# Attention into a token-mixing MLP on one Trainium2 core: one hand-written order of steps exchanged for another

## The chip, the core and the metric

The kernel runs on one NeuronCore of a Trainium2 chip. The core has five engines that run side by side, each with its own queue of instructions in program order: TensorE (PE in the profile, with its weight loads as PEld) multiplies matrices into PSUM; VectorE (DVE), ScalarE (ACT) and GpSimd (POOL) work elementwise; SyncE (SP) issues transfers. GpSimd, SyncE and ScalarE can all issue DMAs. An engine waits for another through semaphores.

The metric is the device time of one execution in microseconds. Before the change it is 104.38 us, the median of three runs (104.2, 104.38 and 105.15). One more execution was taken with the profiler: 104.42 us.

## What is computed

Eight batches, eight heads, 576 rows and head size 64. Thirty-two learned queries `p` pack the keys and values of each head (first softmax), the real queries attend to the packed result (second softmax), and the output, put back to 576 rows of 512, goes through a token-mixing MLP.

```python
def sm_attn(qq, kk, vv):
    s = scale * np.matmul(qq, kk.transpose(0, 1, 3, 2))
    s = s - np.max(s, axis=-1, keepdims=True)
    a = np.exp(s)
    a = a / (np.sum(a, axis=-1, keepdims=True) + 1e-09)
    return np.matmul(a, vv)
p_packed = sm_attn(p, k, v)
out = sm_attn(q, p_packed, p_packed)
# x: (batch, 576, 8 * 64)
wq = x @ w_q
wk = x @ w_k
W_tok = (1 / sqrt(64)) * np.einsum('bsd,btd->bst', wq, wk)
mixed = np.einsum('bst,btd->bsd', W_tok, x)
return np.maximum(mixed, 0.0) @ w_out
```

Inputs and output are fp32; the kernel multiplies in bf16. It never forms `x` or the 576 x 576 matrix `W_tok`: it works with the packed products.

## The kernel before

The kernel has no loops over data in its body. It is a list of small steps, and a string `ORDER` (lines 13 to 57) names every step of all eight batches in the order in which the program issues them. The loop at lines 601 to 622 reads the string and calls one function for each name. An engine therefore does its own steps in the order of the string, and what one step needs from another engine makes it wait. Nothing reorders them.

A name reads `STEP.batch.part@engine=banks`: `RL.5.0@V` is step RL of batch 5, part 0, on VectorE (`V`; `A` is ScalarE, `P` GpSimd, `S` SyncE), and `=6,7` are the PSUM banks that a product goes to. There are eight banks; a product must wait until the step that reads the bank's earlier content is done. Steps without a letter have a fixed engine: products run on TensorE, `LD` on GpSimd's DMA queue, `ST`, `STF`, `STH` on SyncE's unless marked `@P` or `@A`.

What a batch goes through, in order of data:

- `LD.k`, `LD.v`, `LD.q`: loads through GpSimd's queue, cast from fp32 to bf16 on the way (lines 154 to 182). `k0` comes as `h0` and `g0`, `q0` and `q7` as two halves (`r`, `q`). Four buffers each (`NL`). `LD.O` loads `w_out`. Each load waits, on GpSimd, for the transfer that was issued eight before it.
- `KT` (VectorE): the keys transposed in blocks; `S1` (32 matmuls): scores of the packed queries; `X1` (ScalarE): their exponentials, in one buffer; `TE` (VectorE): these transposed.
- `PV` (36 matmuls): the weighted values and, through the ones that `SET.v0` to `SET.v3` write, the sums; `RC`, `PP`, `PT` (VectorE): reciprocal, normalized packed result, its transpose.
- `QK`, `QKE`, `QD`: the packed result times `w_q` and `w_k`, its eviction, and a copy on GpSimd.
- `QV` (VectorE): the queries transposed; `S2` (matmuls), `X2` (ScalarE): scores and exponentials of the second softmax, in parts `.0` to `.3`; `RS`, `RR` (VectorE): row sums and reciprocals, with `HA` on GpSimd for a first addition in batch 5; `AM` (mostly GpSimd): the normalization.
- `AT`, `AE`: the probabilities transposed on TensorE, and evicted.
- `WKQ`, `WE`, `GM`, `GE`, `Y`, `YE`, `MX` and `MR`, `RL` (or `RLF` by halves) and `RLR`: the mixing, each product with its eviction, ending with the ReLU.
- `OT`: four accumulating matmuls of 512 columns against `w_out` for 128 rows (`.0` to `.3`), and `.4` for the 64th rows of two batches together; `OE`, `OEF`: eviction to the output tile; `ST`, `STF`: its store, 512 KB or 256 KB. The last 128 rows of batch 7 are cut in two column parts (`OH`, `OEH`, `STH`), with the bounds in `OHC` (line 11).

`WARM.n=b` puts n times 128 columns of fp32 matmuls without use into bank b, as a filler while TensorE has nothing to do. `HOLD.v7` is a tiny transfer on SyncE's queue that waits for v7's landing, so that the stores behind it on that queue start after the loads.

The steps around the change: at the start, batch 0 runs alone with fillers, and batch 1's first scores begin. In the middle, `OT` of earlier batches is put between the steps of later ones. At the end, stores wait in SyncE's and GpSimd's queues.

Of the kernel before, what the change touches and what calls it, by code (L numbers as in the profile page):

```python
# [23 lines left out]
RS.1.2@V RR.1.2@V S2.1.1=2,3 X2.1.0@A RS.1.0@V RR.1.0@V WARM.1=6 PV.2.0=6,7 PV.2.1 X2.1.1@A RS.1.1@V RC.2@V  # L24
LD.v3 QD.1@P AM.1.2@P AT.1.2=4 RR.1.1@V AM.1.0@P WARM.5=5 AT.1.0=5 AM.1.1@P LD.k4 PP.2.0@V AE.1.2@A PP.2.1@V
PT.2@V QK.2=4 AE.1.0@A QKE.2@A QD.2@P QV.2.2@V LD.q3 LD.v4 AT.1.1=0 AE.1.1@A WKQ.1.0=2,3 WKQ.1.2 WKQ.1.1
WE.1.0@V S2.2.2=6,7 WE.1.1@A X2.2.2@A S2.2.3=4,5 X2.2.3@A GM.1=1 OT.0.0=2,3 GE.1@V Y.1=6,7 OT.0.1 YE.1@A
# [10 lines left out]
HOLD.v7 MR.3=0,1 RC.5@V PP.5.1@V OE.2.1@A MX.3.0=2,3 PP.5.0@V PT.5@V MX.3.1=6,7 RLR.3@A RL.3.0@A OT.3.4=0
RL.3.1@A AT.4.2=1 AE.4.2@A OEF.3.4@A QV.5.2@V AT.4.3=5 AE.4.3@V ST.1.4@P QK.5=4 QKE.5@V QD.5@P S2.5.2=2,3
X2.5.2@A KT.6.2@V S2.5.3=6,7 X2.5.3@A HA.5@P WKQ.4.0=0,1 WKQ.4.2 LD.q7 WKQ.4.1 WE.4.2@A OT.3.0=2,3  # L40
S1.6=4,5,6,7 X1.6.0@A GM.4=0 GE.4@V TE.6.0@V LD.r7 OT.3.1 X1.6.1@A TE.6.1@V Y.4=0,1 OE.3.0@A RS.5.4@V RR.5.4@V
PV.6.0=4,5 YE.4@A PV.6.1 MX.4.0=6,7 RC.6@V RL.4.0@A PP.6.0@V AM.5.3@P PP.6.1@V PT.6@V MX.4.1=2,3 AM.5.2@P
# [10 lines left out]
WE.7.1@A STF.6.2 OT.6.0=6,7 OT.6.1 GM.7=0 OE.6.0@V OT.5.1 OE.5.0@V ST.5.1@P GE.7@A Y.7=4,5 OT.6.3 OEF.6.3@V
ST.6.0 STF.6.3 YE.7@A ST.5.0 MR.7=6,7 RLR.7@A MX.7.0=4,5 RLF.7.0.1@A RLF.7.0.0@V MX.7.1=2,3 RLF.7.1.0@A
OT.7.4=0 OEF.7.4@A ST.7.4 RLF.7.1.1@V OT.7.1=6 OEF.7.1@V OT.7.0=7 STF.7.1 OT.7.2=1 OEF.7.0@A OH.7.0=0 STF.7.0
OEF.7.2@A STF.7.2 OEH.7.0@V STH.7.0 OH.7.1=5 OEH.7.1@A STH.7.1@A
"""


# [1 line left out]
def kernel(  # L61
# [46 lines left out]
    def bank(n, shape, dt=fp32):  # L108
        if isinstance(n, list):
            assert n[1] == n[0] + 1  # L110
            ap = ps_all[:, n[0]:n[1] + 1].rearrange("a k n -> a (k n)")
# [12 lines left out]
        return ap.rearrange(f"a ({' '.join(names)}) -> a {' '.join(names)}", **dims)

    def copy(eng, o, i):
        if eng == "A":
            nc.scalar.activation(o, i, COPY)  # L128
        elif eng == "P":
            nc.gpsimd.tensor_copy(o, i)  # L130
        else:
            nc.vector.tensor_copy(o, i)  # L132
# [441 lines left out]
    def OH(b, h, eng, bk):  # L574
        n0, n1 = OHC[h]
        ps = T["oh", h] = bank(bk, [n1 - n0])
        for j in range(NJ):
            nc.tensor.matmul(ps, T["relu", b][:, j // 2, j % 2, 3 * P:4 * P], wout[:, j, n0:n1],
                             start=j == 0, stop=j == NJ - 1)
# [71 lines left out]
```

## Time and profile before

| | |
|---|---|
| runs, us | 104.2, 104.38, 105.15 |
| profiled execution, us | 104.42 |
| its span, us | 102.6 |
| granted TensorE clock, mean | 0.993 |
| instructions | 3594 |
| moved by DMA | 25.13 MB, 245 GB/s on average |
| share of 16 DMA engines, GpSimd's queue | 84.3% |
| share of 16 DMA engines, SyncE's and ScalarE's queues | 18.9% and 1.9% |

The span runs from the first to the last instruction of the profiled execution; the profiled time holds 1.8 us more that lie around it. Times in the views are counted from the span's start. A transfer's queue time isn't an engine's busy time: an engine is not counted as busy while it issues or waits. Matmul ends are modelled, and matmuls overlap, so the steps of the chain of waits tell better what a product costs than the length of its row.

### The profile page before, as it was taken

How to read it: one execution, taken by the hardware profiler on the slowest of the kernel's cores; microseconds unless marked ns; L12 is line 12 of the kernel's file. 1: busy time of each engine (PE TensorE's matmuls, PEld its weight loads, DVE VectorE, ACT ScalarE, POOL GpSimd, SP SyncE). 2: the span in 40 equal slices, each digit the busy share in tenths (PEclk: the TensorE clock that was granted, in tenths of full speed). 3: DMA queues.
4: the chain of work that ended last, by engine and by line, in shares of the span. 5: the costliest groups of instructions: out<-in, count | busy, mean ns of one | idle time of the engine just before them, and what ended most of it. 6: DMA issues, size and time to landing. Idle time of an engine off the chain costs nothing.

```text
span 102.6 us, 3594 instructions
## 1 busy us (share of the span) xinstructions
PE 93.2 (91%) x1536; PEld 55.1 (54%) x1536; DVE 73.5 (72%) x140; ACT 65.0 (63%) x111; POOL 53.1 (52%) x83
## 2 busy tenths in 40 slices
PE   5998999998699999999998899989999999999930
PEld 3896555465265633755636557544757565643420
DVE  4164376957979479888697979499999979249420
ACT  1320415178754767849977979887989897726430
POOL 5971877993039929724459493649724009300000
PEclk9999999999999999999999999999999999999997
DMA  1999999999999999999999999999999999997893
GB/s 18 234 230 207 211 215 209 207 210 213 203 212 207 214 209 209 213 210 207 212 210 208 211 212 204 216 211 205 250 250 387 412 413 409 417 388 294 346 370 127
DMA packets 13567, 25.13 MB, mean 245 GB/s; under 512 B 1072, under 2 KB 6448, under 8 KB 13552
## 3 DMA queue, kind: packets, MB, share of 16 engines
q0 software_dynamic: 9936, 17.04, 84.3%
q1 hardware_dynamic: 3056, 7.41, 18.9%
q10 hardware_dynamic: 560, 0.46, 1.9%
q8 instruction: 12, 0.20, 0.7%
q14 instruction: 3, 0.02, 0.1%
HBM read 30.15 MB, written 9.44 MB: 386 GB/s over the span
## 4 chain that ended last, share of the span: by engine, by line
PE 64%; DVE 9%; ACT 8%; DMA 7%; POOL 4%; issue 3%; DVEq 0%; POOLq 0%; ACTq 0%
PE ps L540 26%; PE ps L617 9%; DMA k_sb<-in_k_dram 7%; PE ps L373 5%; PE ps L315 4%; ACT e1T L293 4%; POOL a L405 4%; PE ps L282 3%; PE ps L419 3%; PE ps L446 3%; PE ps L467 3%; DVE rs L394 2%; PE ps L441 2%; PE ps L336 2%; DVE kT L237 2%
## 5 line engine op out<-in xcount | busy, mean ns | idle before, releaser
L540 PE MATMUL ps<-wout,relu 128*128 128x512 bf16 x124 | 30.6, 380 | 0.0
L405 POOL TENSOR_TENSOR a<-e,rr 128x256 bf16<-128x256 f32 (+2 forms) x18 | 19.5, 1099 | 16.4 <-DVE rr L399 6.4
L617 PE MATMUL ps<-o 128*128 128x128 f32 (+3 forms) x76 | 20.0, 410 | 1.2 <-DVE o L135 1.2
L540 PEld LDWEIGHTS <-relu 128*128 128x128 bf16 x124 | 10.7, 98 | 11.7 <-issue 1.1
L128 ACT ACTIVATE o<-ps 128x1024 f32<-128x1024 f32 (+2 forms) x13 | 11.3, 870 | 5.4 <-PE ps L540 5.2
L617 PEld LDWEIGHTS ps<-o 128*128 128x128 f32 x76 | 11.8, 217 | 5.2 <-issue 3.6
L503 ACT ACTIVATE relu<-ps 128x1024 bf16<-128x1024 f32 (+1 forms) x14 | 12.9, 966 | 1.1 <-PE ps L492 1.1
L293 ACT ACTIVATE e1T<-ps 128x576 bf16<-128x576 f32 x16 | 9.8, 655 | 5.2 <-PE ps L282 4.6
L378 ACT ACTIVATE e<-ps 128x256 f32<-128x256 f32 (+2 forms) x19 | 11.2, 622 | 2.5 <-PE ps L373 2.4
L394 DVE TENSOR_REDUCE rs<-e 128x16 f32<-128x512 f32 (+2 forms) x13 | 10.9, 841 | 2.3 <-ACT e L378 2.2
L173 POOL DMA_DIRECT2D v_sb<-in_v_dram x16 | 10.0, 629 | 4.2 <-DMA v_sb<-in_v_dram 1.6
L237 DVE STREAM_TRANSPOSE kT<-k_sb 128x1152 uint32<-128x1152 uint32 (+1 forms) x9 | 11.0, 1226 | 1.4 <-DMA k_sb<-in_k_dram 1.3
L237 DVE STREAM_TRANSPOSE qT<-q_sb 128x1152 uint32<-128x1152 uint32 (+1 forms) x10 | 11.0, 1104 | 0.0
L132 DVE COPY o<-ps 128x1024 f32<-128x1024 f32 (+2 forms) x7 | 6.7, 977 | 5.2 <-PE ps L540 2.7
L237 DVE STREAM_TRANSPOSE e<-e1T 128x288 uint32<-128x288 uint32 x16 | 7.4, 468 | 3.1 <-ACT e1T L293 2.6
L128 ACT ACTIVATE aT<-ps 128x128 bf16<-128x128 f32 (+2 forms) x11 | 5.0, 464 | 5.7 <-PE ps L419 3.3
L128 ACT ACTIVATE wkq<-ps 128x448 bf16<-128x448 f32 (+1 forms) x10 | 7.2, 729 | 1.8 <-PE ps L446 1.7
L315 PE MATMUL ps<-v_sb,e 64*64 64x192 bf16 x288 | 7.5, 245 | 0.8 <-DVE e L237 0.5
L315 PEld LDWEIGHTS <-e 64*64 64x64 bf16 x288 | 5.9, 107 | 2.6 <-DVE e L237 2.0
L373 PEld LDWEIGHTS <-qT 64*128 64x128 bf16 x320 | 5.4, 94 | 2.6 <-DVE qT L237 1.5
L446 PE MATMUL ps<-aT,pqk 128*128 128x256 bf16 (+1 forms) x48 | 6.8, 246 | 0.0
L373 PE MATMUL ps<-ppT,qT 64*128 64x64 bf16 x320 | 6.6, 190 | 0.1
(70 smaller groups left out, 131.5 us busy)
## 6 DMA issues: line engine op xcount, KB each, us to landing
v_sb<-in_v_dram POOLq DMA_DIRECT2D x16, 288.0 KB, 14.5
out_dram<-o SPq DMA_DIRECT2D x9, 512.0 KB, 8.9
k_sb<-in_k_dram POOLq DMA_DIRECT2D x7, 576.0 KB, 14.0
q_sb<-in_q_dram POOLq DMA_DIRECT2D x6, 576.0 KB, 13.5
out_dram<-o POOLq DMA_DIRECT2D x4, 512.0 KB, 9.0
out_dram<-o SPq DMA_DIRECT2D x5, 256.0 KB, 3.0
...
```

Of the source, the lines that this page charges most:

```text
L128: nc.scalar.activation(o, i, COPY)
L173: nc.gpsimd.dma_start(v_bufs[b % NL][halves(i), 0:7:2], src)
L237: nc.vector.transpose(o, i)
L293: nc.scalar.activation(e1T[:, x], T["s1", b][x].rearrange("a c m -> a m c"), EXP, scale=scale)
L315: nc.tensor.matmul(T["pv", b][halves(cc), i], lhsT, rhs, start=n == 0, stop=n == R - 1, skip_group_check=True)
L373: nc.tensor.matmul(ps[:, y, t - t0, i], lhsT, rhs, start=e == 0, stop=e == 1)
L378: nc.scalar.activation(e2[:, t0:t1].rearrange("a t (i y n) -> a y (t i) n", i=2, y=2), T["s2", b, c].rearrange("a y t i n -> a y (t i) n") ...
L394: nc.vector.tensor_reduce(rs[:, t0 * H:t1 * H], src, axis=AX, op=ADD)
L405: e.tensor_tensor(a2[:, t0:t1].rearrange("a t i (u l) -> a (t i u) l", l=L), e2v(b, c), T["rr", b][:, t0 * H:t1 * H].to_broadcast((P, (t1 ...
L503: nc.scalar.activation(o, i, RELU)
L540: nc.tensor.matmul(ps, lhsT, wout[:, j, :], start=j == 0, stop=j == NJ - 1)
L617: nc.tensor.matmul(bank(int(bk), [w]), warm[:, 0:P], rhs, start=True, stop=True)
```

## The change

Only `ORDER` and `OHC` differ. Every step of the computation is still there, with the same shapes; the order in the string, the engine of some evictions, and many banks are different. What changes, by stage:

- Start: the mask, the memsets of ones and the loads of k2, v1, q1, v2 stand differently among each other on GpSimd. Batch 0's parts 0 and 1 exchange places in `S2` to `AT`. `S1.1` comes before `WKQ.0`, `X1.1` before `WE.0`; `S1.2` before `GM.0`. `GE.0` goes to VectorE, `YE.0` to ScalarE, `RLR.0` to VectorE, `QKE.1` to ScalarE, `AE.1.0` to VectorE, `WE.1.0` to ScalarE. `TE.2.1` moves behind `PP.1.1`. The fillers add up to 77 units of 128 columns instead of 69; behind `QK.1` it is `WARM.6` instead of `WARM.3`.
- Loads: the order of the transfers on GpSimd's queue stays, but for the two halves of q7 (`r7` first) and the steps between them: `AM.2` before `LD.q4`, `AM.3` before `LD.v6`, `AM.4` and `QD.4` before `LD.v7`, `HA.5` and the loads of q7 before `QD.5`.
- Middle: `GM.2`, `Y.2` and `MX.2.1` come before the rest of batch 1's `OT`; `YE.2` and `RL.2.1` go to VectorE, `RLR.2` and `QKE.3` to ScalarE. `QK.5` moves behind `Y.4`; `AT.4` before `OT.3.4`; `GE.5` and `AE.6.2` go from ScalarE to VectorE.
- Stores: `ST.2.1` and, late, `ST.3.0`, `ST.5.1` and `ST.5.4` are on GpSimd's queue; before, `ST.1.1`, `ST.0.1`, `ST.3.0` early and `ST.5.1` late. SyncE's queue has the others in another order.
- End: batch 7's `AT`, `WKQ`, the last `OT` of batches 5 and 6 and their evictions change places and engines; the two column parts of the last rows exchange names.

The core of the diff (the start, the middle, and the end of the string):

```diff
-OHC = (0, 384), (384, 512)
+OHC = (384, 512), (0, 384)
...
-KT.1.2@V AM.0.1@P WARM.3=2 AT.0.1=7 AE.0.1@A AE.0.0@V WKQ.0.0=2,3 WKQ.0.2 WE.0.0@A LD.q2 WKQ.0.1 KT.2.2@V
-S1.1=0,1,4,5 WE.0.1@A GM.0=6 X1.1.0@A TE.1.0@V GE.0@A WARM.2=7 Y.0=2,3 YE.0@V S1.2=0,1,6,7 MR.0=2,3 X1.1.1@A
-TE.1.1@V MX.0.0=4,5 X1.2.0@A LD.O PV.1.0=0,1 TE.2.0@V PV.1.1 X1.2.1@A TE.2.1@V RC.1@V LD.k3 PP.1.0@V PP.1.1@V
-PT.1@V MX.0.1=6,7 QV.1.2@V RLR.0@A QK.1=2 QKE.1@V RL.0.0@A WARM.3=3 S2.1.2=4,5 S2.1.0=0,1 RL.0.1@A X2.1.2@A
+RR.0.0@V AM.0.0@P WARM.3=2 AT.0.0=2 KT.1.2@V S1.1=0,1,4,5 X1.1.1@A X1.1.0@A AE.0.0@V WKQ.0.0=6,7 WKQ.0.2
+WE.0.0@A KT.2.2@V WKQ.0.1 WARM.2=3 S1.2=2,3,4,5 WE.0.1@A GM.0=0 LD.q2 LD.O TE.1.0@V TE.1.1@V GE.0@V SET.v3@P
+LD.k3 X1.2.0@A TE.2.0@V LD.v3 WARM.2=1 Y.0=6,7 PV.1.0=2,3 PV.1.1 RC.1@V PP.1.0@V PP.1.1@V X1.2.1@A TE.2.1@V
+YE.0@A PT.1@V MR.0=0,1 RLR.0@V MX.0.0=4,5 RL.0.0@A MX.0.1=6,7 RL.0.1@A QK.1=2 QKE.1@A QD.1@P QV.1.2@V WARM.6=3
...
-WE.2.2@A OT.1.2=4,5 OT.1.3 PP.3.0@V PT.3@V QK.3=6 OE.1.1@A LD.q5 KT.4.2@V S1.4=0,1,2,3 GM.2=7 OT.1.0=4,5
-X1.4.1@A LD.k6 GE.2@A QKE.3@V X1.4.0@A QV.3.2@V TE.4.1@V Y.2=2,3 YE.2@A S2.3.2=6,7 X2.3.2@A S2.3.3=0,1
-X2.3.3@A MX.2.0=2,3 TE.4.0@V RL.2.0@A MR.2=6,7 RLR.2@V OT.1.1 MX.2.1=6,7 RL.2.1@A OE.1.0@A PV.4.0=0,1 QD.3@P
+RC.3@V PP.3.0@V OT.1.2=6,7 WE.2.2@A GM.2=0 GE.2@A KT.4.2@V S1.4=2,3,4,5 X1.4.1@A PP.3.1@V PT.3@V X1.4.0@A
+Y.2=0,1 YE.2@V OT.1.3 OE.1.1@A MX.2.1=0,1 QV.3.2@V RL.2.1@V LD.q5 TE.4.1@V QK.3=4 LD.k6 TE.4.0@V S2.3.2=2,3
+QKE.3@A X2.3.2@A S2.3.3=6,7 X2.3.3@A MX.2.0=4,5 OT.1.0=2,3 RS.3.4@V RR.3.4@V MR.2=0,1 PV.4.0=6,7 PV.4.1 RC.4@V
...
-OT.4.2=0,1 GM.5=4 TE.7.1@V OT.4.3 AT.6.3=5 X1.7.0@A TE.7.0@V GE.5@A OE.4.1@A AM.6.2@P AT.6.2=4 ST.2.0 Y.5=6,7
-YE.5@A ST.0.0 ST.3.1 PV.7.0=2,3 QV.7.1@V AE.6.3@V QV.7.0@V AE.6.2@A QD.6@P PV.7.1 RC.7@V PP.7.0@V PP.7.1@V
+TE.7.1@V X1.7.0@A OT.4.2=2,3 GM.5=4 GE.5@V TE.7.0@V QV.7.0@V OT.4.3 ST.1.1 OE.4.1@A AT.6.3=5 AM.6.2@P AT.6.2=4
+AE.6.2@V ST.0.0 Y.5=6,7 AE.6.3@V ST.4.0 PV.7.0=0,1 PV.7.1 RC.7@V PP.7.0@V QV.7.1@V YE.5@A MR.5=2,3 RLR.5@A
...
-RR.7.2@V MR.6=2,3 OT.5.3 RLR.6@V RL.6.0@V RL.6.1@A OE.5.1@A ST.4.1 AM.7.0@P OT.5.0=2,3 AM.7.2@P AT.7.0=4
-AE.7.0@A AT.7.1=5 AE.7.1@V AT.7.2=6 AE.7.2@V OT.6.2=0,1 OEF.6.2@A QD.7@P WKQ.7.0=4,5 WKQ.7.2 WKQ.7.1 WE.7.0@A
+AM.7.1@P RLR.6@V AM.7.0@P OT.5.3 OE.5.1@A RR.7.2@V OT.5.0=6,7 AT.7.1=4 RL.6.0@V AE.7.1@V AT.7.0=5 AE.7.0@V
+OT.6.2=0,1 OEF.6.2@V ST.3.0@P QD.7@P AM.7.2@P AT.7.2=2 WKQ.7.0=4,5 WKQ.7.1 AE.7.2@A STF.6.2 WKQ.7.2 WE.7.1@V
+WE.7.0@A OT.5.1 OE.5.0@A ST.5.1@P ST.5.4@P GM.7=0 OT.6.0=2,3 OT.6.1 OE.6.0@A ST.5.0 GE.7@V Y.7=4,5 OT.6.3
```

More of the change, by code (lines that the diff above doesn't have):

```diff
@@ L23 @@
-PT.1@V MX.0.1=6,7 QV.1.2@V RLR.0@A QK.1=2 QKE.1@V RL.0.0@A WARM.3=3 S2.1.2=4,5 S2.1.0=0,1 RL.0.1@A X2.1.2@A
[L24 to L27, printed above, removed]
@@ L38 @@
[L38 to L42, printed above, removed]
@@ L53 @@
[L53 to L56, printed above, removed]
+LD.g0 LD.v0 LD.r0 LD.q0 LD.k1 NC.0@V PX.0@V NC.1@A PX.1@V SET.aff@P SET.idb@V KT.0.0@V KT.0.1@V WC.1@P WC.0@P
@@ new lines @@
+PP.2.0@V PP.2.1@V PT.2@V QK.2=4 QKE.2@A AT.1.1=0 AE.1.1@A AE.1.0@V WKQ.1.0=6,7 WKQ.1.2 LD.k4 WE.1.0@A WKQ.1.1
+WE.1.1@A QV.2.2@V S2.2.2=2,3 X2.2.2@A S2.2.3=4,5 X2.2.3@A GM.1=1 GE.1@V OT.0.0=6,7 Y.1=2,3 YE.1@A OT.0.1
+OE.0.0@A MX.1.1=0,1 RS.2.4@V RL.1.1@A MR.1=4,5 RR.2.4@V QD.2@P KT.3.2@V OT.0.2=2,3 RLR.1@A OT.0.3 S1.3=6,7,0,1
+X1.3.0@A LD.q3 OE.0.1@V LD.v4 AM.2.2@P TE.3.0@V X1.3.1@A AM.2.3@P AT.2.2=4 LD.q4 LD.k5 OT.1.4=5 AT.2.3=6
+OEF.1.4@A MX.1.0=2,3 TE.3.1@V LD.v5 AE.2.3@V PV.3.0=0,1 AE.2.2@A RL.1.0@A PV.3.1 WKQ.2.0=4,5 WKQ.2.1 WKQ.2.2
@@ new lines @@
+LD.r7 X1.6.0@A OT.3.1 OE.3.0@A LD.q7 Y.4=0,1 ST.2.1@P TE.6.1@V TE.6.0@V YE.4@A ST.0.1 QK.5=2 QKE.5@A QD.5@P
+PV.6.0=4,5 PV.6.1 RS.5.4@V RR.5.4@V MX.4.0=6,7 RL.4.0@A RC.6@V PP.6.1@V MX.4.1=0,1 RL.4.1@A PP.6.0@V PT.6@V
+AM.5.3@P QV.6.2@V OT.3.2=2,3 OT.3.3 OE.3.1@V QK.6=5 QKE.6@A ST.3.1 S2.6.2=6,7 S2.6.3=0,1 X2.6.2@A X2.6.3@A
+MR.4=4,5 RLR.4@V AM.5.2@P AT.5.2=6 AE.5.2@A AT.5.3=7 AE.5.3@A OT.4.0=2,3 OT.4.1 OE.4.0@A WKQ.5.0=4,5 WKQ.5.2
+KT.7.2@V ST.1.0 RS.6.4@V WKQ.5.1 WE.5.2@A S1.7=0,1,6,7 ST.3.4 QD.6@P ST.2.0 RR.6.4@V AM.6.3@V X1.7.1@A
@@ L57 @@
+STF.7.2 STF.7.0 OH.7.0=5 OEH.7.0@A OEH.7.1@V STH.7.1@A STH.7.0
 """
```

36 lines of the change are left out of this document (18 added, 18 removed).

## The prediction

> **What bounds the kernel now.** I read the page's engine and DMA rows first, then the windows, then the end of the chain of waits. From the page, its busy times, its GB/s slices (2.56 us each) and its chain by engine:
>
> ```profile
> PE 93.2 (91%) x1536; PEld 55.1 (54%) x1536; DVE 73.5 (72%) x140; ACT 65.0 (63%) x111; POOL 53.1 (52%) x83
> ...
> GB/s 18 234 230 207 211 215 209 207 210 213 203 212 207 214 209 209 213 210 207 212 210 208 211 212 204 216 211 205 250 250 387 412 413 409 417 388 294 346 370 127
> ...
> PE 64%; DVE 9%; ACT 8%; DMA 7%; POOL 4%; issue 3%; DVEq 0%; POOLq 0%; ACTq 0%
> ```
>
> TensorE (PE) holds 64% of the chain. The GB/s row has two plateaus: about 210 while the loads arrive, and about 410 from slice 30 (77 us) on, when only stores flow. Up to about 77 us the arrival of the loads times each batch, and TensorE fills the rest with products of earlier batches. The windows (stretch, its length, busy time of PE, PEld, DVE, ACT and POOL, the clock, DMA share, GB/s) tell what binds afterwards:
>
> ```profile
> 70.00:80.00 10.00, 10.00 (x201) 6.30 (x199) 9.86 (x13) 8.78 (x16) 5.55 (x7) 1.00 1.11 283
> ...
> 78.70:84.30 5.60, 5.55 (x136) 3.84 (x134) 4.87 (x12) 5.32 (x12) 0.00 (x0) 1.00 1.03 410
> 84.30:88.00 3.70, 3.70 (x32) 1.83 (x30) 3.06 (x8) 2.97 (x5) 3.18 (x5) 1.00 1.02 409
> 88.00:91.00 3.00, 3.00 (x30) 1.77 (x29) 0.38 (x2) 1.52 (x4) 0.35 (x1) 1.00 1.04 420
> 91.00:94.00 3.00, 2.98 (x31) 1.19 (x29) 2.88 (x3) 1.07 (x4) 0.00 (x0) 1.00 0.76 303
> ```
>
> From 70 us on TensorE is never free for long, and VectorE (DVE) is busy 9.86 of 10 us in 70 to 80. The DMA share falls to 0.76 in 91 to 94 us, so the stores don't bind the last ten microseconds. The end of the chain of waits (start, length, what):
>
> ```profile
> 94.03 3.63 PE ps L540 x16
> 97.66 0.67 PE ps L578 x4
> ...
> 98.40 0.56 DVE o L132
> ```
>
> The last products run without a break to 98.3 us. An eviction, the last store and its landing make the rest of the 102.6 us span. So the end is TensorE's backlog plus some 4 us. Time is won only where TensorE idles less between 40 and 82 us, and lost wherever a feeder falls behind it there.
>
> **The start: batch 1's queries come later.** S1.1 and its exponentials move ahead of WKQ.0 and WE.0. TE.2.1 moves from before RC.1 to behind PP.1, and RLR.0 goes from ScalarE to VectorE, ahead of QV.1. The filler behind QK.1 grows from WARM.3 to WARM.6. Timeline (start, length, engine, line, what; in brackets the idle time before and its releaser), and two rows of the chain of waits:
>
> ```profile
> 24.98 0.94 PE L315 MATMUL ps<-v_sb,e 64*64 64x192 bf16 x36 [0.24 <-ACT e1T L293]
> 28.47 0.78 PE L373 MATMUL ps<-ppT,qT 64*128 64x64 bf16 x40
> ...
> 24.96 1.02 DVE L237 STREAM_TRANSPOSE e<-e1T 128x288 uint32<-128x288 uint32 x2 [0.34 <-ACT e1T L293]
> ...
> 27.08 1.34 DVE L237 STREAM_TRANSPOSE qT<-q_sb 128x1152 uint32<-128x1152 uint32 x1
> ...
> 49.58 0.42 DVE L505 TENSOR_SCALAR rem<-ps 128x256 bf16<-128x256 f32 x1 [0.58 <-PE ps L498]
> ...
> 13.15 1.49 PE ps L617 x4
> ...
> 27.21 0.41 PE ps L336 x8
> ```
>
> PV.1 waited 0.24 us for batch 1's and 2's exponentials; I credit all of it. Behind PV.1 on VectorE, QV.1 (27.08) now has half of the 1.02 (0.51, TE.2.1) and a 0.42 (RLR.0) ahead of it: 0.93 - 0.24 - 0.1 for overlapping starts = 0.6 us later, so it ends near 29.0. PT.1 has only TE.2.1 in front, 0.51 - 0.24 = 0.27, so QK.1 starts at 27.21 + 0.27 = 27.48; with its 0.41 and 1.49 of filler (the 13.15 row is a WARM.6) TensorE is free only near 29.3. Starts overlap a little, so S2.1 moves from 28.47 to about 29.2: **+0.75**. Bounds: +0.3 if PV.1 comes 0.5 earlier still, +1.0 if the credit fails.
>
> On GpSimd the memset of v2's ones now stands between QD.0 and the loads of v2, ahead of AM.0.2:
>
> ```profile
> 13.53 0.60 POOL L206 MEMSET v_sb<- 128x576 uint32 x1
> 17.53 0.62 POOL L405 TENSOR_TENSOR a<-e,rr 128x256 bf16<-128x256 f32 x1 [0.34 <-DVE rr L399]
> ...
> 39.92 0.48 PE L282 MATMUL ps<-kT,pT 32*32 32x288 bf16 x32
> ```
>
> 0.60 less the 0.34 of idle time is 0.26, and the longer filler WARM.8 (two units more, at 1.49/6 each = 0.5) lies over it: free; without that cover it is 0.26. The loads of k2, v1, q1 are issued a little later but keep their order, and the load queue has work without a pause (GB/s row), so they land as before. The mask and the ones of v1 and v3 are memsets that only change places: free. From S2.1 to S1.3 each step waits for the one ahead: S1.3, at 39.92 now, inherits +0.75.
>
> **Batch 2's products ahead of batch 1's.** Before S2.3 TensorE did OT.1.2, OT.1.3, QK.3, S1.4, GM.2, OT.1.0, Y.2; now OT.1.2, GM.2, S1.4, Y.2, OT.1.3, MX.2.1, QK.3. OT.1.0 leaves the path, MX.2.1 enters. YE.2 goes to VectorE, ahead of QV.3.
>
> ```profile
> 37.86 0.22 PE ps L492 x2
> ...
> 44.19 0.92 ACT L128 ACTIVATE wkq<-ps 128x896 bf16<-128x896 f32 x1 [0.93 <-PE ps L446]
> ...
> 23.81 0.42 DVE L486 TENSOR_SCALAR y<-ps 128x256 bf16<-128x256 f32 x1
> ...
> 46.67 1.37 DVE L237 STREAM_TRANSPOSE qT<-q_sb 128x1152 uint32<-128x1152 uint32 x1
> ...
> 48.54 0.67 PE ps L373 x32
> ```
>
> One OT is 3.63/4 = 0.91. The path loses 0.91 and gains 0.22: -0.69. GM.2 now follows WE.2.2 (0.92) with one OT (0.91) as its only cover: +0.1. TensorE would thus reach S2.3 at +0.75 - 0.69 + 0.1 = +0.16. But Y.2 and YE.2 (0.42) come before QV.3, and QV.3 starts at about 47.25, not 46.67; S2.3.3 also needs the bank that OE.1.1 empties. I take **+0.4** at S2.3.3 (48.54 now), between +0.16 and +0.75. The 0.69 is owed again behind it (OT.1.0 before PV.4), which the next stall must cover.
>
> ```profile
> 54.46 0.62 PE L419 MATMUL ps<-idb,a 128*128 128x128 bf16 x8 [0.45 <-POOL a L405]
> 57.22 0.49 PE L282 MATMUL ps<-kT,pT 32*32 32x288 bf16 x32 [0.32 <-DVE kT L237]
> 68.14 0.94 PE L315 MATMUL ps<-v_sb,e 64*64 64x192 bf16 x36 [0.47 <-DVE e L237]
> ...
> 62.94 0.34 PE ps L336 x8
> ```
>
> AT.3.3 idled 0.45 for AM.3.3; the owed work fills this, and AT.3.3 keeps about +0.45 as its VectorE chain does. The 0.32 before S1.5 remains, for KT.5 is as late as TensorE. In batch 4 AT.4 moves ahead of OT.3.4 and waits for AM.4.2, but S2.5 waits for QV.5 anyway: free while QV.5 is late. QK.5 (0.34) moves from before S2.5 into the 0.47 idle before PV.6: -0.1 after what the later TE.6 takes. PV.6 stands at **+0.35**.
>
> **VectorE's full stage.** GE.5 and AE.6.2 go from ScalarE to VectorE, which has no idle time there; QV.7.1 moves between PP.7.0 and PP.7.1.
>
> ```profile
> 77.77 0.31 ACT L128 ACTIVATE g<-ps 128x128 bf16<-128x128 f32 x1
> ...
> 66.73 0.29 DVE L132 CAST g<-ps 128x128 bf16<-128x128 f32 x1 [1.31 <-PE ps L467]
> 42.76 0.27 DVE L132 CAST aT<-ps 128x128 bf16<-128x128 f32 x1
> 81.07 0.31 DVE L237 STREAM_TRANSPOSE ppT<-pp 128x128 uint32<-128x128 uint32 x1
> 81.30 1.19 DVE L505 TENSOR_SCALAR relu<-ps 128x1024 bf16<-128x1024 f32 x1
> ...
> 82.11 0.41 PE L373 MATMUL ps<-ppT,qT 64*128 64x64 bf16 x16
> 82.86 0.53 PE L373 MATMUL ps<-ppT,qT 64*128 64x64 bf16 x24
> ```
>
> 0.29 + 0.27 = 0.56 more on VectorE; what leaves ScalarE (0.31 for GE.5) helps no one, since the waits there end with VectorE. RL.5.0 (81.30 + 1.19 = 82.49) empties the banks of S2.7.0, which starts near 83.0 (behind the first 8 of the 24 matmuls of the 82.86 row): cover 0.50. So 0.56 - 0.50 = 0.06 if TensorE is on time, and the whole 0.56 on top of VectorE's lag if TensorE isn't. With both 0.35 late: 0.4. I take +0.2 for the stage, a sum of **+0.55**. [...]
>
> **Stores and tail.** ST.3.0, ST.5.1 and ST.5.4 are issued late by GpSimd, ST.3.0 and QD.7 ahead of AM.7.2.
>
> ```profile
> 84.53 2.63 POOL L405 TENSOR_TENSOR a<-e,rr 128x512 bf16<-128x512 f32 x3 [6.35 <-ACT y L484]
> 87.10 0.29 POOL L130 COPY pqk<-pqk 128x128 bf16<-128x128 bf16 x1
> 87.68 0.66 POOL L561 DMA_DIRECT2D out_dram<-o  x1 [0.29 <-ACT o L128]
> ```
>
> AM.7 ran to 87.16; one issue (0.66) and QD.7 (0.29) ahead of AM.7.2 make it 0.95 later. AT.7.2 now stands behind OT.6.2, 0.91 of cover: hidden, and up to 0.95 late if the cover is gone. WKQ.7, GM.7, Y.7 and MX.7 keep the same products around them in another order, WE.7.1, GE.7 and YE.7 go to VectorE, which is nearly idle there (0.38 of 3 us in 88 to 91): 0. The last product is cut as before, 384 columns and then 128, with the two stores' queues exchanged: 0. Moving 0.75 MB of stores (ST.3.0, ST.5.4) to later and ST.5.0 ahead of ST.6.0 fills room that the DMA has at 91 us: 0. The two queues together moved 410 GB/s (78.7 to 84.3), SP's alone 409 (84.3 to 88): a second queue adds no rate. [...]
>
> **Sum.** The profiled execution took 104.42 us (span 102.6 and 1.8 around it; the median of the runs is 104.38). 104.42 + 0.75 - 0.40 + 0.20 = 104.97, so **105.0**. The runs spread from 104.2 to 105.15, so 1% (below 103.3, above 105.4) is about what a measurement can tell from no change.
>
> **Rivals.**
> Slower: the lag is not absorbed. Mechanism: QV.3 is held by YE.2 while VectorE is itself 0.75 late, so S2.3 gets 0.75 + 0.42 = +1.17 and every later query step queues behind it; the full stage adds 0.06 to 0.56. 104.42 + 1.17 + 0.2 = 105.8. It decides once QV.3 starts later than about 47.7. For it: VectorE's 9.86 of 10. Against: the 0.69 that leaves the path. With AM.7.2's cover gone too, up to 106.7.
> Faster: TensorE makes up the start, and the three stalls quoted (0.45 + 0.32 + 0.47 = 1.24) are all filled by moved products: 103.2. For it: QK.5 does fit the 0.47. Against: two of the three stalls are waits on chains through VectorE, which gets more work.
> No effect: S1.3 waits for k3's landing and the backlog hides the rest, and the stores' new queues do nothing: 104.4. For it: the 0.76 DMA share. Against: S1.3 had no idle time before it that could hide a lag.
>
> **Chances.** Forecast case 0.42, its own range 104.3 to 105.6, of which about a sixth (0.07) lies above 105.4; slower rival 0.35; faster 0.13; no effect 0.10. Faster by over 1%: 0.13. Within 1%: 0.35 + 0.10 = 0.45. Slower by over 1%: 0.35 + 0.07 = 0.42. The range is 103.6 (most of the faster rival left out, 0.1) to 106.2 (the slower one's end left out, 0.08).
>
> **What would show it.** Right: S2.1 near 29.2 with filler or QV.1 ending last before it; S1.3 near 40.7; YE.2 directly before QV.3; S2.3.3 near 48.9; no idle time left before PV.6; RL.5.0 ending last before S2.7.0, near 83.5; the last product near 98.9. Wrong: S2.1 at 28.5 or earlier, S1.3 still at 39.9, or a tail longer than the 16.2 us from S2.7.1 to the end of the products, with AT.7.2 or a store's landing ending a wait there.

## The result: 105.01 us, and a profile with a stall that no step of the prediction names

| | before | changed |
|---|---|---|
| median of 21 runs each, us | 104.60 | 105.01 |
| lowest and highest, us | 104.12, 105.15 | 104.60, 105.54 |
| profiled execution, us | 104.42 | 105.54 |
| its span, us | 102.6 | 103.8 |

The ratio of the changed kernel to the one before is 1.0045, with a 95% interval of 1.0028 to 1.0061: 0.4 us slower, inside the 1% that was called no change, and 0.01 us from the forecast. The kernel before took 104.60 us in this comparison, 0.18 more than the profiled execution on which the forecast builds, so a measured change of +0.41 us stands beside a forecast one of +0.55. The profiled execution of the changed kernel is the highest of its 21 runs, so a second one was taken (the first experiment below).

The page of the changed kernel: busy time, share of the span and count of each engine; GB/s in 40 slices; the chain of waits by engine.

```profile
PE 93.1 (90%) x1520; PEld 54.4 (52%) x1536; DVE 72.9 (70%) x142; ACT 64.8 (62%) x109; POOL 53.0 (51%) x83
...
GB/s 8 233 229 209 212 211 212 207 210 210 208 216 202 212 211 209 214 209 205 215 210 207 213 210 207 218 207 204 260 265 400 411 411 409 374 384 261 381 257 156
...
PE 49%; DMA 21%; issue 6%; ACT 6%; POOL 6%; DVE 6%; SPq 1%; ACTq 0%; POOLq 0%; DVEq 0%
```

The two plateaus are those of before. "Issue", time in which an engine waited for nothing that the profile shows, doubled from 3% of the chain to 6% (and 16 records of products are missing: 1520 products beside 1536 weight loads). That share alone proves little: e12 below, which has no stall, has 6% too. Of the 21% for DMA, 13% are the transfer of queries, for which VectorE waits here; in the second profile the chain has no DMA. The timeline (start, length, engine, line, what; in brackets the idle time before and its releaser) shows the start on VectorE and TensorE, then the middle:

```profile
26.96 0.39 DVE L505 TENSOR_SCALAR rem<-ps 128x256 bf16<-128x256 f32 x1
27.74 1.38 DVE L237 STREAM_TRANSPOSE qT<-q_sb 128x1152 uint32<-128x1152 uint32 x1 [0.40 <-DMA q_sb<-in_q_dram]
...
27.43 1.56 PE L617 MATMUL ps<-o 128*128 128x512 f32 x4
29.18 0.51 PE L373 MATMUL ps<-ppT,qT 64*128 64x64 bf16 x22 [0.19 <-DVE qT L237]
...
40.55 0.48 PE L282 MATMUL ps<-kT,pT 32*32 32x288 bf16 x32
...
46.98 0.42 DVE L486 TENSOR_SCALAR y<-ps 128x256 bf16<-128x256 f32 x1 [0.59 <-PE ps L477]
47.32 1.37 DVE L237 STREAM_TRANSPOSE qT<-q_sb 128x1152 uint32<-128x1152 uint32 x1
...
57.66 0.48 PE L282 MATMUL ps<-kT,pT 32*32 32x288 bf16 x32 [0.32 <-DVE kT L237]
...
68.60 0.60 PE L315 MATMUL ps<-v_sb,e 64*64 64x192 bf16 x18 [0.27 <-DVE e L237]
69.82 0.60 PE L315 MATMUL ps<-v_sb,e 64*64 64x192 bf16 x18 [0.61 <-issue]
70.35 0.61 PE L492 MATMUL ps<-wkq,y 64*128 64x512 bf16 x4
```

S2.1 starts at 29.18 (28.47 before), S1.3 at 40.55 (39.92), QV.3 at 47.32 right behind YE.2, S1.5 at 57.66 (57.22). So far these are the forecast's marks. Then PV.6, one row of 36 products before, is cut in two: after 18 products TensorE idles 0.61 us, and no releaser is named. MX.4 behind it is at 70.35 against 69.01 before: 1.34 us late, where S1.5 was 0.44 late. The row of before:

```profile
69.01 0.60 PE L492 MATMUL ps<-wkq,y 64*128 64x512 bf16 x4
```

VectorE's full stage and the end add nothing. A row of the windows (stretch, length, busy time of PE, PEld, DVE, ACT and POOL, clock, DMA share, GB/s), and two of the timeline:

```profile
70.00:80.00 10.00, 9.84 (x173) 5.78 (x168) 9.39 (x15) 7.99 (x12) 4.30 (x4) 1.00 1.11 278
```

```profile
82.85 1.19 DVE L505 TENSOR_SCALAR relu<-ps 128x1024 bf16<-128x1024 f32 x1
...
84.19 0.54 PE L373 MATMUL ps<-ppT,qT 64*128 64x64 bf16 x24
```

VectorE is busy 9.39 of 10 us (9.86 before), though two evictions were added: it waits for a later TensorE. RL.5.0 ends at 82.85 + 1.19 = 84.04. Of the 24 products the first 8 are those of S2.7.2; S2.7.0, which needs RL.5.0's banks, starts 0.13 behind the first of them, near 84.32, so 0.28 us of cover are left. The row at 84.19 is 1.33 later than before (82.86), so all of the lag is already there at MX.4.

**One clock for all profiles.** S1.0, the first scores, starts at another moment in each execution, depending on the first keys (in e6 it waits 0.91 us for VectorE's transpose of them) and on the first filler (in e5 that runs to 11.06 us). Counted from its last weight load, profiles of like kernels agree to some hundredths. The table gives, worked out from the rows of the timeline, where S1.0 lies, and how much later or earlier than in the kernel before the later marks come from there (before: S2.1 18.40, S1.5 47.15, MX.4 58.94, end of the span 92.58 us behind S1.0; a mark is its first product).

| kernel | S1.0, us | S2.1 | S1.5 | MX.4 | end | measured ratio |
|---|---|---|---|---|---|---|
| changed, first profile | 10.24 | +0.54 | +0.27 | +1.17 | +0.95 | 1.0045 |
| e1_after_again | 10.25 | +0.32 | +0.05 | +0.90 | +0.69 | 1.0065 |
| e2_old_start | 10.21 | +0.03 | -0.18 | +0.44 | +0.22 | 1.0058 |
| e3_new_start | 9.78 | +0.31 | -0.07 | -0.07 | -0.14 | 0.9999 |
| e4_dve_back | 9.71 | +0.30 | +0.01 | +0.56 | +0.53 | 1.0079 |
| e5_eight_more | 11.17 | +0.31 | +0.02 | +0.06 | -0.14 | 1.0068 |
| e6_before_ten_less | 9.90 | 0.00 | -0.01 | +0.64 | +1.33 | 1.0105 |
| e7_before_qk5 | 9.63 | +0.08 | +0.07 | +0.75 | +0.46 | 1.0070 |
| e8_stores_later | 9.55 | +0.29 | +0.02 | +0.65 | +0.43 | 1.0050 |
| e9_shift_late | 10.52 | +0.26 | +1.38 | +1.42 | +1.20 | 1.0055 |
| e10_old_start_shift | 10.09 | +0.35 | +0.16 | +0.18 | -0.03 | 1.0040 |
| e11_short_filler | 9.87 | +0.05 | -0.23 | +0.64 | +0.43 | 1.0027 |
| e12_wide_filler | 9.71 | +0.30 | +0.03 | +0.06 | -0.16 | 1.0075 |

The ratios of the experiments go by their own runs of the kernel before, whose median was 104.06 to 104.15 us. The profile of before, from which the marks are counted, took 104.42 us, some 0.3 us more than those medians, and both profiles of the changed kernel are the highest of their runs (105.54 of 21, 105.30 of 9). So the marks tell where the time goes within a profile, and the ratios how much it is.

### The profile page after: what moved, and what is told of

Its sections match the earlier page's. It is cut to its first block, busy times and chain, and to the rows that moved or that the text cites. A ratio compares the mean times of both kernels' runs of the same rounds, so it can differ in the third digit from the quotient of the medians.

```text
span 103.8 us, 3577 instructions
## 1 busy us (share of the span) xinstructions
PE 93.1 (90%) x1520; PEld 54.4 (52%) x1536; DVE 72.9 (70%) x142; ACT 64.8 (62%) x109; POOL 53.0 (51%) x83
## 4 chain that ended last, share of the span: by engine, by line
PE 49%; DMA 21%; issue 6%; ACT 6%; POOL 6%; DVE 6%; SPq 1%; ACTq 0%; POOLq 0%; DVEq 0%
PE ps L540 25%; DMA q_sb<-in_q_dram 13%; DMA o<-in_moe_w_q_dram 8%; PE ps L373 5%; PE ps L315 4%; PE ps L419 3%; PE ps L446 3%; DVE qT L237 3%; ACT e1T L293 2%; POOL a L405 2%; PE ps L441 2%; PE ps L282 2%; ACT wkq L128 2%; PE ps L467 2%; PE ps L492 2%
## 5 line engine op out<-in xcount | busy, mean ns | idle before, releaser
L540 PE MATMUL ps<-wout,relu 128*128 128x512 bf16 x111 | 29.3, 380 | 0.8 <-issue 0.2
L617 PE MATMUL ps<-o 128*128 128x128 f32 (+3 forms) x76 | 21.5, 427 | 1.2 <-DVE o L135 1.2
L128 ACT ACTIVATE o<-ps 128x1024 f32<-128x1024 f32 (+2 forms) x14 | 12.8, 911 | 6.3 <-PE ps L540 6.0
L503 ACT ACTIVATE relu<-ps 128x1024 bf16<-128x1024 f32 (+1 forms) x13 | 12.1, 959 | 2.5 <-PE ps L492 2.0
L132 DVE COPY o<-ps 128x512 f32<-128x512 f32 (+2 forms) x6 | 5.1, 847 | 3.5 <-PE ps L540 2.2
L128 ACT ACTIVATE aT<-ps 128x128 bf16<-128x128 f32 (+2 forms) x10 | 4.1, 419 | 4.5 <-PE ps L414 3.5
```

The lines of the kernel that those rows point to most:

```text
L503: nc.scalar.activation(o, i, RELU)
L540: nc.tensor.matmul(ps, lhsT, wout[:, j, :], start=j == 0, stop=j == NJ - 1)
L617: nc.tensor.matmul(bank(int(bk), [w]), warm[:, 0:P], rhs, start=True, stop=True)
```

## The first four experiments: where the time is

**The changed kernel again** (nothing edited).

> The changed kernel once more, nothing edited, for a second profile beside the first one. Theory (the lag of the start, some 0.7 us at S2.1, is carried on as 0.45 us to the end): time 0.45 us above the kernel before (ratio 1.004), S2.1 again near 29.2 us, and the 0.61 us of issue time inside PV.6 at 69.8 us is an accident of the first profile and is gone, so that the products end near 99.0 us. Rival (the stall inside PV.6 belongs to the new order): it is there again, at the same place, and the products end near 99.9 us. Of QV.1: if q1's landing at 27.7 us was jitter of one execution, it lands near 26.6 us here, and TE.2.1 and RLR.0 alone hold QV.1.

Measured: 104.71 us, ratio 1.0065 (1.0044 to 1.0086). The timeline of this second profile:

```profile
27.00 0.39 DVE L505 TENSOR_SCALAR rem<-ps 128x256 bf16<-128x256 f32 x1
27.31 1.36 DVE L237 STREAM_TRANSPOSE qT<-q_sb 128x1152 uint32<-128x1152 uint32 x1
...
27.48 1.56 PE L617 MATMUL ps<-o 128*128 128x512 f32 x4
28.97 0.72 PE L373 MATMUL ps<-ppT,qT 64*128 64x64 bf16 x36
...
68.40 0.60 PE L315 MATMUL ps<-v_sb,e 64*64 64x192 bf16 x18 [0.28 <-DVE e L237]
69.56 0.60 PE L315 MATMUL ps<-v_sb,e 64*64 64x192 bf16 x18 [0.55 <-issue]
```

The stall inside PV.6 is there again after 18 products, 0.55 us: no accident, the rival was right. Here QV.1 starts right behind RLR.0, without the 0.40 us that it waited for q1's landing in the first profile, and S2.1 (28.97) follows the filler WARM.6 (27.48 + 1.56) with no idle time: the filler sets S2.1.

**Start and rest exchanged.** Everything ahead of S2.1 was taken from the other kernel; one place of each edit:

```diff
 # e2: the changed kernel
-YE.0@A PT.1@V MR.0=0,1 RLR.0@V MX.0.0=4,5 RL.0.0@A MX.0.1=6,7 RL.0.1@A QK.1=2 QKE.1@A QD.1@P QV.1.2@V WARM.6=3
+PT.1@V MX.0.1=6,7 QV.1.2@V RLR.0@A QK.1=2 QKE.1@V RL.0.0@A WARM.3=3 QD.1@P RL.0.1@A
...
 # e3: the kernel before
-PT.1@V MX.0.1=6,7 QV.1.2@V RLR.0@A QK.1=2 QKE.1@V RL.0.0@A WARM.3=3 S2.1.2=4,5 S2.1.0=0,1 RL.0.1@A X2.1.2@A
+YE.0@A PT.1@V MR.0=0,1 RLR.0@V MX.0.0=4,5 RL.0.0@A MX.0.1=6,7 RL.0.1@A QK.1=2 QKE.1@A QD.1@P QV.1.2@V WARM.6=3
+S2.1.2=4,5 S2.1.0=0,1 X2.1.2@A
```

> The changed kernel with everything ahead of S2.1 as in the kernel before (loads, memsets, order of TE.2.1, RLR.0, WARM.3), and the rest as changed. Theory (the start costs it all): S2.1 at 28.5 us, 0.45 us less than the changed kernel, so level with the kernel before (ratio 1.000). Rival (what comes behind the start costs it, or absorbs any lag): ratio 1.004, as the changed kernel.

> The kernel before with everything ahead of S2.1 as in the changed kernel, and the rest as before. Theory (the start costs it all): S2.1 at 29.2 us, and 0.45 to 0.7 us above the kernel before (ratio 1.004 to 1.007; the higher one if only the new order of batch 2's products takes in some of the lag). Rival (the rest costs it): ratio 1.000.

Measured: 1.0058 (1.0035 to 1.0080) with the old start, 0.9999 (0.9985 to 1.0012) with the new one. My theory fell: the start's +0.31 at S2.1 (e3) is gone by S1.5, and the rest costs the time without any lag of the start. Both kernels with the changed rest stall in PV.6, the one with the old rest doesn't.

**VectorE's stage undone.**

```diff
-GE.5@V
+GE.5@A
...
-AE.6.2@V
+AE.6.2@A
```

> The changed kernel with GE.5 and AE.6.2 back on ScalarE. Theory by the trace of the changed kernel (VectorE's full stage is covered there by TensorE's own work): no change, 0.45 us above the kernel before (ratio 1.004). Rival as predicted (the full stage costs 0.2 us and up to 0.56): 0.2 to 0.45 us less than the changed kernel, ratio 1.000 to 1.002.

Measured: 1.0079 (1.0051 to 1.0107), no gain. From MX.4 to the end this profile takes 0.19 us longer than e1 (in the table, -0.03 against -0.21), so the two evictions are better on VectorE, by a little. The predicted cost isn't there.

## The stall: instructions that arrive in blocks

The page of the first profile has a line for a queue of its own, and a window around 68 us (67.3 to 68.4) shows one packet of it (queue, kind: packets, MB, share of 16 engines):

```profile
q8 instruction: 12, 0.20, 0.7%
```

```profile
q8 instruction: 1, 0.02, 5.5%
```

Twelve packets of 16 KB (0.20 MB in all), and TensorE's stream is 1536 weight loads and 1536 products, 3072 = 12 x 256 instructions. So a packet holds 256 instructions, 128 weight loads and their products, if these are its instructions (an inference, which the next runs test). That twelve packets give just the whole number is chance: kernels with 1526 to 1544 loads, below, have twelve too. The step of 128 loads does stand in the traces. Counted back in such steps from the load behind the pause, the 1119th, there are twelve, which begin at the 95th, the 223rd and so on up to the 1503rd load, and each holds the start of one packet: 0.19 to 4.04 us behind the load that begins it in the first profile, 0.62 to 3.68 us in the profile of before. So none of these packets starts before TensorE, by this count, is in the block ahead of the one it brings.

New theory: TensorE asks for a block when it enters the one before it. Where it runs through 128 loads faster than the packet arrives, it waits with no releaser in the profile. The eighth packet of each profile but e12's, with the weight load that starts the next block by this theory (the 1119th of the stream):

| kernel | loads in all | packet, us | 1119th load, us | pause before it, start to start | behind the packet's end |
|---|---|---|---|---|---|
| before | 1536 | 65.76 to 66.70 | 68.42 | 0 | 1.72 |
| changed | 1536 | 67.39 to 68.36 | 69.81 | 0.93 | 1.46 |
| e1 | 1536 | 67.22 to 68.20 | 69.56 | 0.88 | 1.36 |
| e2 | 1534 | 66.71 to 67.67 | 69.09 | 0.67 | 1.42 |
| e4 | 1536 | 66.48 to 67.42 | 68.68 | 0.58 | 1.26 |
| e6 | 1526 | 66.75 to 67.70 | 69.19 | 0.78 | 1.49 |
| e7 (1120th load) | 1536 | 66.57 to 67.53 | 68.79 | 0.73 | 1.26 |
| e8 | 1536 | 66.23 to 67.21 | 68.61 | 0.66 | 1.40 |
| e11 | 1534 | 66.55 to 67.52 | 68.99 | 0.96 | 1.47 |
| e3 | 1538 | 65.31 to 66.29 | 68.06 | 0.07 | 1.77 |
| e5 | 1544 | 66.59 to 67.57 | 69.41 | 0 | 1.85 |
| e9 | 1544 | 67.35 to 68.33 | 70.12 | 0 | 1.79 |
| e10 | 1542 | 65.63 to 66.78 | 68.53 | 0.07 | 1.75 |

In every profile with the stall it comes at the same load of the stream (one later in e7), and TensorE goes on 1.26 to 1.49 us behind the packet's end; in those without it TensorE gets there 1.72 us or more behind the packet. At the other blocks, counted in steps of 128 loads, it gets there 1.57 us or more behind, and in no profile does TensorE idle anywhere else without a releaser, except for 0.16 us in places of profiles that miss records of products. What differs is when the packet comes. QK.5's eight loads stand behind S2.5 in the changed kernel, and so the point at which the block is asked for falls behind S2.5's wait for the queries (0.53 us between two loads there); the last 128 loads up to the cut then take only 5.0 us. The 1119th load is the nineteenth of PV.6, hence 18 products before the pause. Four kernels test this.

**Eight more loads ahead of S1.0 in the changed kernel; ten fewer in the kernel before.** The same columns of filler in more or fewer products; each of these fp32 products counts as two weight loads (four more of them in e5 make 1544 loads of 1536, five fewer in e6 1526).

```diff
 # e5: the changed kernel
-WARM.22.128=0
+WARM.22.112=0
...
 # e6: the kernel before
-WARM.22.128=0
+WARM.22.166=0
```

> The changed kernel with the first filler cut into 26 products of 112 columns in place of 22 of 128: the same columns, eight more weight loads, all of them before S1.0, so every later instruction stands eight loads further on in TensorE's stream. Theory (TensorE's instructions arrive in blocks of 16 KB, 128 products with their weight loads each, and in PV.6 it waits for a block that was asked for only 5.0 us earlier): with the cut moved by eight loads the same block is asked for ahead of S2.5's wait, TensorE takes over 6.0 us to reach its end, the stall inside PV.6 is gone, and the time falls by 0.5 to 0.9 us, to level with the kernel before or 0.3 us below it (ratio 0.997 to 1.001). Rival (the stall belongs to PV.6, to its banks or its data, or to DMA traffic at 68 us): it stays, and the ratio stays at 1.005.

> The kernel before with its first filler cut into 17 products of 166 columns in place of 22 of 128: the same columns, ten weight loads fewer, nothing else. Theory (blocks of instructions): the cut moves behind S2.5's wait for the queries, as in the changed kernel, and TensorE reaches the end of the block 5.3 us later, so a stall of 0.2 to 0.5 us with no releaser appears near MX.4 or the end of PV.6, at 68.6 us, and the time is 0.2 to 0.5 us above the kernel before (ratio 1.002 to 1.005). Rival (the stall belongs to the order of the changed kernel's steps): no stall, ratio 1.000.

PV.6 in the timeline of e5, and then of e6:

```profile
69.30 0.94 PE L315 MATMUL ps<-v_sb,e 64*64 64x192 bf16 x36 [0.28 <-DVE e L237]
```

```profile
67.96 0.77 PE L315 MATMUL ps<-v_sb,e 64*64 64x192 bf16 x28 [0.47 <-DVE e L237]
69.19 0.36 PE L315 MATMUL ps<-v_sb,e 64*64 64x192 bf16 x8 [0.46 <-issue]
```

Both behave as the theory says. In e5 PV.6 is whole again, and MX.4 is +0.06 against e1's +0.90. In e6, whose steps behind the filler are those of the kernel before, the stall appears, after 28 products in place of 18: ten loads fewer ahead of it, ten products later in the step. It belongs to the count of instructions, not to PV.6's data or banks. The measured times go only half with it. e6 is at 1.0105 (1.0078 to 1.0132), more than the 0.64 at MX.4: another 0.69 us comes behind MX.4, which the theory doesn't say. All of it lies behind the last product; the row of before, and then of e6:

```profile
97.49 1.04 PE L578 MATMUL ps<-wout,relu 128*128 128x384 bf16 x8
```

```profile
97.97 1.04 PE L578 MATMUL ps<-wout,relu 128*128 128x384 bf16 x8
```

From there to the end of the span it is 4.12 us before (98.53 to 102.65) and 4.80 in e6 (99.01 to 103.81). What holds the last stores there stays open. e5 is at 1.0068 (1.0045 to 1.0090), no gain: its filler of 26 products lasts 0.92 us longer than the 22 of e1, so S1.0 is at 11.17 in place of 10.25, and that lag is carried in full to S1.5 and on. From S1.0 to the end it is 0.14 us shorter than the kernel before.

**QK.5 alone moved in the kernel before; the stores alone moved back in the changed one.** With QK.5, QKE.5 goes to ScalarE, and the banks of QK.5 and MX.4 change. The pieces of the string that differ:

```diff
 # e7: the kernel before
-QK.5=4 QKE.5@V QD.5@P
...
-PV.6.0=4,5 YE.4@A PV.6.1 MX.4.0=6,7
+QK.5=6 PV.6.0=4,5 YE.4@A QKE.5@A QD.5@P PV.6.1 MX.4.0=2,3
...
-MX.4.1=2,3
+MX.4.1=6,7
...
 # e8: the changed kernel
-Y.4=0,1 ST.2.1@P TE.6.1@V TE.6.0@V YE.4@A ST.0.1
+Y.4=0,1 TE.6.1@V TE.6.0@V YE.4@A
...
-QV.6.2@V
+QV.6.2@V ST.2.1
...
-S1.7=0,1,6,7
+S1.7=0,1,6,7 ST.0.1@P
```

> The kernel before with QK.5, QKE.5 and QD.5 moved from ahead of S2.5 to ahead of PV.6 (QKE.5 on ScalarE behind YE.4), one part of the change alone. As predicted (QK.5 fits the 0.47 us of idle time before PV.6): 0.1 us less than the kernel before, ratio 0.999. Theory (QK.5's eight loads stand behind S2.5 now, so the cut of the block does too): a stall of 0.3 to 0.6 us with no releaser inside PV.6, ratio 1.003 to 1.006.

> The changed kernel with the stores ST.2.1 and ST.0.1 issued where the kernel before issues them, behind QV.6 and S1.7, in place of before PV.6. The block of instructions that TensorE waits for started 3.6 us after it was asked for, against 2.7 us in the kernel before. Rival (the two early stores delay it): it starts some 0.7 us earlier, and the stall inside PV.6 and the time fall by 0.5 us (ratio 1.001). Theory (the place of the cut decides, the stores don't): the stall stays at 0.3 to 0.6 us, ratio 1.005.

The timeline of e7, QK.5 and PV.6:

```profile
67.26 0.41 PE L336 MATMUL ps<-wqk,ppT 64*64 64x128 bf16 x7
67.78 0.60 PE L315 MATMUL ps<-v_sb,e 64*64 64x192 bf16 x18
68.78 0.60 PE L315 MATMUL ps<-v_sb,e 64*64 64x192 bf16 x18 [0.41 <-issue]
```

QK.5 does fill the idle time before PV.6, but PV.6, which waits for VectorE, starts no earlier for it: 67.78 - 9.63 = 58.15 us behind S1.0, against 68.14 - 10.07 = 58.07. Then it stalls after 18 products: MX.4 +0.75, ratio 1.0070 (1.0047 to 1.0092). That one move makes the kernel before about as slow as the whole change does. The stores do nothing to it: e8 keeps the stall (0.34 idle, 0.66 between the loads), ratio 1.0050 (1.0031 to 1.0068).

## The last four: the cut moved otherwise, and a shorter filler

**Eight more loads behind QK.1** (e9 in the changed kernel, e10 with the old start, built as e2), **and the short filler alone** (e11, which keeps the cut).

```diff
 # e9
-WARM.6=3
+WARM.2.43=3
...
 # e10
-WARM.3=3
+WARM.2.52=3
...
 # e11
-WARM.6=3
+WARM.3=3
```

> The changed kernel with the filler behind QK.1 in six narrow products (256 columns in all) in place of two wide ones (768 columns): eight more weight loads ahead of S2.1 and a shorter filler, nothing else. Theory (the cut between two blocks of instructions behind S2.5's wait makes the stall in PV.6): the block is asked for ahead of S2.5's wait, there is no stall in PV.6, and the time is 0.6 to 1.0 us below the changed kernel, so level with the kernel before or up to 0.3 us below it (ratio 0.997 to 1.000). Rival (the earlier experiment with eight more loads lost its stall only because its start was 0.9 us late): the stall stays, ratio 1.004 to 1.006.

> The changed kernel with everything ahead of S2.1 as in the kernel before, and the filler behind QK.1 in five narrow products (256 columns in all) in place of one of 384: eight more weight loads. Theory: no stall in PV.6, and the new order of batch 2's products is then worth the 0.2 us that it gained at S1.5 when the start was the old one: 0.2 to 0.4 us below the kernel before (ratio 0.996 to 0.998). Rival (the stall's cost comes back elsewhere, behind PV.6): ratio 1.003 to 1.006.

> The changed kernel with WARM.3 in place of WARM.6 behind QK.1, as in the kernel before: a shorter filler, and two weight loads fewer. The filler ends last before S2.1 when the queries land in time, so S2.1 comes some 0.3 us earlier. Theory (the lag of the start is taken in before S1.5, the stall in PV.6 makes the time): the stall stays and the time is as that of the changed kernel (ratio 1.005). Rival (as predicted: what S2.1 loses is carried on to the end): 0.3 us below the changed kernel, ratio 1.002.

Measured: e9 104.83 us, 1.0055 (1.0020 to 1.0091, without the run of 106.08 us); e10 104.42 us, 1.0040 (1.0012 to 1.0067); e11 104.33 us, 1.0027 (1.0007 to 1.0048). The stall is gone in e9 and e10 and stays in e11, as expected. The times of e9 and e10 are misses; e10's lies where its rival put it. Windows of e9's profiled execution, the slowest of its ten (106.08 us; clock third from the right):

```profile
29.00:30.00 1.00, 1.00 (x43) 0.95 (x42) 0.07 (x1) 0.49 (x2) 0.00 (x0) 0.77 1.08 206
30.00:32.00 2.00, 2.00 (x9) 0.51 (x3) 1.90 (x5) 0.88 (x2) 1.04 (x2) 0.50 1.17 204
32.00:33.00 1.00, 1.00 (x25) 0.90 (x28) 0.00 (x0) 0.00 (x0) 0.62 (x1) 0.52 1.27 210
33.00:35.00 2.00, 2.00 (x36) 1.12 (x28) 1.33 (x6) 0.28 (x1) 1.02 (x2) 1.00 1.16 216
```

After the narrow filler the granted clock fell to 0.50 for over three of the next four microseconds, and S1.5 came 1.38 late. Five of e9's ten runs have a mean clock of 0.983 or 0.984 and took 105.16 to 106.08 us, five have 0.996 or more and took 103.91 to 104.51. So the narrow filler lost on the clock what the cut gained. The five with the higher clock have a median of 104.17 us, level with the 104.10 of the kernel before, as the theory has it; since they are picked by their clock afterwards, this agrees with it and proves nothing. In e10 two of twelve runs have 0.984; its filler also took 1.31 us in place of 0.91, so that S2.1 was +0.35, which ate the gain of the middle. e10's median lies 0.3 us above the kernel before, though its profile (104.41 us) is level with that of before from S1.0 on. The profile of before is the reason: at 104.42 us it took longer than each of the 27 runs of before beside e10 (103.85 to 104.41, median 104.10). Where those runs are shorter, no trace shows. In e11, S2.1 and S1.5 come 0.27 and 0.28 earlier than in e1: in the new middle the filler's time is carried on, as predicted, and its ratio is nearer to the rival's 1.002.

**Seven wide products as the first filler of the changed kernel.**

```diff
-WARM.22.128=0
+WARM.18.330=0
```

> The changed kernel with its first filler in seven products of up to 330 columns (2304 columns in all) in place of 22 of 128 (2816 columns): 30 weight loads fewer ahead of S1.0, and a filler that should end before the keys' transposes, where the old one ended 0.6 us behind them. Theory (the cut between two blocks of instructions makes the stall in PV.6): with the cut 30 loads later no block is shorter than 6.5 us, the stall is gone, and with the earlier S1.0 the time is 0.9 to 1.3 us below the changed kernel and 0.2 to 0.7 us below the kernel before (ratio 0.993 to 0.998). Rival (a stall that goes in one place comes back at another, as the measured times of the last two kernels without it suggest): ratio 1.002 to 1.006.

Measured: 104.78 us, 1.0075 (1.0046 to 1.0105), outside both ranges. There is no stall: the 1119th load, in QK.6, starts 3.47 us behind the end of its packet. From S1.0 to the end of the span it is 0.16 us shorter than the kernel before, S1.0 is early (9.71), and the span, 102.1, is the shortest of all profiles. The time isn't: around the span lie 2.26 us in the profiled execution, and 2.73 in one other. The remaining four have 1.75 to 1.90 there, as all other kernels (1.73 to 1.90), but spans of 102.8 to 103.6. The page of e12 counts one packet fewer within the span, and a window from 102.1 to 106 us shows it:

```profile
q8 instruction: 11, 0.18, 0.6%
```

```profile
q8 instruction: 1, 0.02, 2.0%
```

With 30 loads fewer the last cut (the 1503rd load of 1506) falls so late that the twelfth packet starts at 103.33 us, behind the last instruction that the span counts. One could think that the stall of PV.6 came back there, as the rival had it. The trace speaks against this: 2.0% of 16 engines over 3.9 us are 1.25 us, so the packet ends near 104.6 us, later than the whole execution of 104.36 us, and by the count of 128 loads no product stands in its block. What makes e12 slow stays open. No version beat the kernel before.

## Why the prediction was right

The time is right to 0.01 us, the steps are not: errors of both signs cancelled, and the kernel before came out 0.18 us above the figure to which the sum was added. That is luck. By the table, e1 against the kernel before:

| step | forecast | e1 |
|---|---|---|
| start, to S2.1 | +0.75 | +0.32 |
| middle, S2.1 to S1.5 | -0.30 | -0.27 |
| S1.5 to MX.4 | -0.10 | +0.85 |
| MX.4 to the end | +0.20 | -0.21 |
| sum | +0.55 | +0.69 |

- **Start, right mechanism, wrong size.** S2.1 waits for the longer filler or for QV.1, as written. But S1.1's earlier place brings PV.1 forward by 0.45 from S1.0, not by the 0.24 credited; so QV.1 is hardly late, and the filler alone holds S2.1. With the short filler (e11) S2.1 is at +0.05.
- **"They land as before" was wrong once.** In the first profile q1 landed at 27.72 us (26.56 before) and held QV.1 for 0.40 us, which makes +0.54 in place of +0.32. In the second it landed at 27.16 and held nothing. So the first profile's S2.1, at 29.18 close to the forecast's 29.2, is late by 0.32 for the change, 0.22 for q1 and 0.17 for a later S1.0.
- **Loads as the clock of each batch: wrong.** In e5 S1.0 is 0.92 us later than in e1, and S1.5 is 0.89 later, with no wait for k3's or k5's landing. The plateau of 210 GB/s shows a busy queue, not that it sets the pace.
- **The middle was right.** YE.2 runs directly ahead of QV.3, and S2.1 to S1.5 takes 28.48 us against 28.75. What carried over to PV.6 is so much smaller only because the start was. The old middle behind the new start (e3) takes 28.37; I can't say why it takes the lag in as well.
- **QK.5 ahead of PV.6 was the wrong step.** The text said "-0.1 after what the later TE.6 takes"; it costs 0.55 to 0.9 (S1.5 to MX.4 in the profiles with the stall) through the block of instructions, which e7 shows by itself. No view of the profile of before shows a stall of this kind; its page does have the twelve packets, and I didn't ask what they carry. For the other blocks of these two kernels no such pause stands in the rows. In measured time e7 alone carries this (1.0070): the four versions of the changed kernel without the stall took 1.0040 to 1.0075, two with another lag that the profile shows (e5 at S1.0, e9 by the clock) and two without (e10, e12). That its cure would make the changed kernel level with the one before is therefore argued, not shown.
- **VectorE's full stage: nothing, not +0.2.** The cover before S2.7.0 shrank from 0.50 (the forecast's own figure) to 0.28 and was never used up. Undoing the two moves (e4) made that part 0.19 longer. The whole 0.56, which the prediction puts down for a late TensorE, didn't come either: VectorE was about as full as before (9.39 of 10 us), but TensorE was later still.
- **Stores and tail: 0 forecast, 0.2 shorter.** The last products of the changed kernel:

```profile
98.82 1.04 PE L578 MATMUL ps<-wout,relu 128*128 128x384 bf16 x8
```

  From MX.4 to their end it is 29.51 us (70.35 to 99.86), and 29.52 before (69.01 to 98.53): the new order of batch 7 costs and gains nothing. The 0.2 lies behind the last product: all ten profiles with the changed end take 3.91 to 3.93 us from there to the end of the span, the four with the old end 3.84 (e7) to 4.80 (e6), the kernel before 4.12. The changed end is the steadier one; that it is shorter isn't sure.
- **The signs named beforehand.** YE.2 stands directly before QV.3, and S1.3 is near 40.7, as written. Three failed: 0.27 us of idle time stayed before PV.6, RL.5.0 doesn't end last before S2.7.0, and the products end at 99.86 us, not near 98.9.

In the profiles without the stall the changed kernel is about 0.15 us shorter than the kernel before from S1.0 on (e5, e12), which is no difference that these runs can tell.
